# Fused attention and gated MLP on one core: q and k loaded in natural rows, their transposes copied out contiguously, Pool and sync queues in program order

## The chip, the cores and the metric

The kernel runs on one core of a Trainium2 chip. Times are device microseconds of that core, from the first instruction to the last with a little around them; the span in a profile is the stretch between the first and the last recorded instruction. TensorE (PE) multiplies, ScalarE (ACT) and VectorE (DVE) read the results out of PSUM, GpSimd (POOL) works in SBUF only, and SyncE (SP) issues transfers.

## The reference, cut to what matters

There are 8 batches, 8 heads, 512 local and 32 global positions, and a head width of 64. Local queries see the 32 global keys and the local keys at a distance of at most 32; global queries see all keys. The output of the attention, 4352 rows of 512, goes through an MLP of width 2048.

```python
s_ll = scale * np.matmul(q_l, k_l.transpose(0, 1, 3, 2))
mask = np.abs(pos[:, None] - pos[None, :]) <= window        # window = 32
s_ll = np.where(mask, s_ll, -1000000000.0)
s_lg = scale * np.matmul(q_l, k_g.transpose(0, 1, 3, 2))
a_l = sm(np.concatenate([s_lg, s_ll], axis=-1))
out_l = np.matmul(a_l, np.concatenate([v_g, v_l], axis=2))
out_g = np.matmul(sm(scale * np.matmul(q_g, k_all.transpose(0, 1, 3, 2))), v_all)
...
h = x @ w_in
g = h * np.clip(h + 3.0, 0.0, 6.0) / 6.0
out = g @ w_out
```

## The kernel before, in words

**The work is cut into 32 pairs.** A pair `p` is two heads of a batch: batch `b = p // 4`, pair `m = p % 4` of the batch. Heads of a pair share the 128 partitions, 64 each.

- `load_rows` (L93) brings q and k from HBM as fp32. Partition `p` of `kf` and `qf` holds, for each head, the four rows `4p` to `4p + 3`, which lie side by side in HBM: one contiguous run of 1024 bytes for each partition and head. One transfer brings 8 heads of one tensor, 1 MB. The tiles have two buffers.
- `cast_rows` (L121) turns the two heads of a pair into fp16, as `kr` and `qr`, with the fourth `j` of each partition's rows as the outer dimension.
- `emit_T` (L197) transposes `kr` and `qr` on PE in eight 128x128 pieces into one PSUM bank `psT`. Piece `j` holds rows `j, 4 + j, 8 + j, ...`, so that the copies out of PSUM, three on DVE for `kT` (L212) and one on ACT for `qT` (L215), read runs and write every fourth fp16 element.
- `emit_QK` (L220) makes the scores: five small products with the global queries (`psG`, L229) and two PSUM tiles for each head (`psS`, L239), in five chunks of keys. ACT takes the exponential (L242, L244), DVE multiplies with the mask (L245, L247).
- `emit_AV` (L253) multiplies with v, whose tile `vn` has 64 columns of ones beside each head, so that the sums of the softmax arise in the same product (`pav`, L272; `pg` for the global queries, L274). ACT takes the logarithm of the sums (L276) and the exponential of its negative (L279), DVE multiplies (L282). After the last pair of a batch eight DVE multiplications write the global rows `xg` (L292).
- `emit_globals` (L182) transposes the global q and k of a batch (L187) and copies them out on DVE (L190) and ACT (L193).

**The MLP of a batch runs one batch later, in units between the parts of the attention.** `moe_units` (L296) makes 16 units `u1` (four matmuls of 512 columns, L302; a ReLU on ACT, L306; one DVE operation into `gt`, L308) and 16 units `u2` (four matmuls, L317; after every fourth unit a DVE copy `ot`, L321, and a store, L323). `M(n)` issues the next n units. In a pair stand 8 units, in the last of a batch 6 and the rest, so that pairs 0 and 1 of a batch hold the `u1` of the batch before, pairs 2 and 3 its `u2`. After batch 7 its units and those of the 256 global rows run alone.

**What sets the order.** The loop at L368 writes for each pair: loads of the next batch, `emit_T(p + 2)`, the casts of the next batch's pair `m`, `emit_globals(b + 1)` at `m == 1`, one unit, `emit_QK(p + 1)`, four units, `emit_AV(p)` with one unit inside, two units. A scheduler then orders every engine's instructions by its own estimate. It may hoist a transfer on the POOL or SP queue ahead of work written earlier. Weights (`load_w_in` L335, `load_w_out` L340), v (`load_v` L128) and the global q and k (`load_g` L115) come through POOL's queue, which casts fp32 to fp16 on the way; q, k, the v of batch 0 (`load_v0` L135, cast by `cast_v0` L139) and all stores go through SP's. PSUM has 7 general banks (`psp`) and one for `pg`.

Of the kernel before, what the change touches and what calls it, by code (L numbers as in the profile page):

```python
# [14 lines left out]
def kernel(  # L15
# [12 lines left out]
    nc = tc.nc  # L28
    P = 128
# [7 lines left out]
    J = 4  # L37
# [55 lines left out]
    def load_rows(eng, t, src, h0, nh):  # L93
        eng.dma_start(out=t[:, h0:h0 + nh].rearrange("p h j d -> p h (j d)"),  # L94
                      in_=src[h0:h0 + nh].rearrange("h (p j) d -> p h (j d)", j=J))

# [8 lines left out]
    def new_nat(b):  # L105
        f = [natp.tile([P, H, J, D], FP32, tag=t, name=t) for t in ("kf", "qf")]
        nat[b] = (f, {})

    def load_qk(b):
        new_nat(b)  # L110
        for i, src in enumerate((k_l, q_l)):
            load_rows(nc.sync, nat[b][0][i], src[b], 0, H)
# [8 lines left out]
    def cast_rows(b, m, copies):  # L121
        f, r = nat[b]
        r[m] = [natp.tile([P, J, 2, D], FP16, tag=f"{t}{m}", name=f"{t}{m}") for t in ("kr", "qr")]
        for i in range(2):
            copies[i](out=r[m][i],
                      in_=f[i][:, 2 * m:2 * m + 2].rearrange("p h j d -> p j h d"))
# [25 lines left out]
    for i, src in enumerate((k_l, q_l)):  # L152
        load_rows(nc.sync, nat[0][0][i], src[0], 4, 4)
# [43 lines left out]
    def emit_T(p):  # L197
        b, m = divmod(p, NM)
        psT = ps_tile("psT", FP16)
        for w, t in enumerate(nat[b][1][m]):  # L200
            for j in range(J):
# [8 lines left out]
        kv = psT[:, 0:Sl].rearrange("d (j p) -> d j p", j=J)  # L210
        for k0, k1, c0 in SEG:
            nc.vector.tensor_copy(  # L212
                out=kT[:, c0:c0 + k1 - k0].rearrange("d (p j) -> d j p", j=J),
                in_=kv[:, :, k0 // J:k1 // J])
        nc.scalar.copy(  # L215
            out=qT.rearrange("d (p j) -> d j p", j=J),
            in_=psT[:, Sl:2 * Sl].rearrange("d (j p) -> d j p", j=J))
# [32 lines left out]
    xg = [const(f"xg{m}", [P, B, Sg]) for m in range(NM)]  # L250
    pgs = {}

    def emit_AV(p, mid):  # L253
# [29 lines left out]
        if m == NM - 1:  # L283
# [5 lines left out]
            for mm in range(NM):  # L289
                for e in range(2):  # L290
                    r = slice(e * D, (e + 1) * D)
                    nc.vector.tensor_tensor(out=xg[mm][r, b], in0=Rg[r, mm], in1=pg[0:D, mm, e],  # L292
# [134 lines left out]
```

## Time and profile before

| what | value |
|---|---|
| median of 3 runs | 392.61 us (391.6 to 395.03) |
| the profiled execution | 392.18 us, its span 390.5 us |
| span up to the first scores of batch 2 (pair 8) | 98.1 us |
| batches 2 to 6 | 41.5 us each |
| batch 7 | 39.3 us |
| the MLP alone at the end | 45.6 us |
| PE, DVE, ACT, POOL busy | 337.8, 273.8, 270.4, 86.4 us |
| mean granted TensorE clock | 0.989 |

The stages begin where PE issues `psG` of a batch's first pair. A busy PE is not a PE at its peak, since matmuls overlap; where PE waits, the rows of the timeline say for whom, in square brackets. Transfers are split into packets; the view of the transfers counts the packets of each queue in a stretch of time, q0 being POOL's queue and q1 being SP's.

### The profile page before, as it was taken

How to read it: one execution, taken by the hardware profiler on the slowest of the kernel's cores; microseconds unless marked ns; L12 is line 12 of the kernel's file. 1: busy time of each engine (PE TensorE's matmuls, PEld its weight loads, DVE VectorE, ACT ScalarE, POOL GpSimd, SP SyncE). 2: the span in 40 equal slices, each digit the busy share in tenths (PEclk: the TensorE clock that was granted, in tenths of full speed). 3: DMA queues.
4: the chain of work that ended last, by engine and by line, in shares of the span. 5: the costliest groups of instructions: out<-in, count | busy, mean ns of one | idle time of the engine just before them, and what ended most of it. 6: DMA issues, size and time to landing. Idle time of an engine off the chain costs nothing.

```text
span 390.5 us, 6834 instructions
## 1 busy us (share of the span) xinstructions
PE 337.8 (87%) x2560; PEld 186.0 (48%) x2560; DVE 273.8 (70%) x628; ACT 270.4 (69%) x479; POOL 86.4 (22%) x134
## 2 busy tenths in 40 slices
PE   0346686899998999899989999899989998999994
PEld 0224454455454545455545555454545454544472
DVE  4648787966886588857876587668865887276271
ACT  1259896966897589856994799668975897275070
POOL 4057424913321162116211520022000000000000
PEclk9999979999999999999999999999999999999998
DMA  8999999982970195219201660029001100200202
GB/s 168 208 225 274 274 247 179 238 249 62 90 222 10 60 108 164 60 55 98 31 1 43 76 62 2 27 62 87 3 8 60 44 0 2 81 29 0 81 29 54
DMA packets 72274, 36.82 MB, mean 94 GB/s; under 512 B 47408, under 2 KB 67888, under 8 KB 72240
## 3 DMA queue, kind: packets, MB, share of 16 engines
q0 software_dynamic: 44656, 9.25, 26.8%
q1 hardware_dynamic: 27584, 27.14, 22.7%
q8 instruction: 20, 0.33, 0.3%
q14 instruction: 14, 0.11, 0.1%
HBM read 36.70 MB, written 8.91 MB: 117 GB/s over the span
## 4 chain that ended last, share of the span: by engine, by line
PE 41%; ACT 20%; DVE 17%; DMA 11%; issue 5%; SPq 5%; POOL 0%; ACTq 0%
PE po L317 28%; DMA gz_79<-in_k_g_dram 6%; PE psH L302 6%; DVE kT L212 4%; ACT qT L215 4%; ACT Ln L276 4%; SPq L137 4%; PE pav L272 3%; DVE gt L308 3%; DMA qf<-in_q_l_dram 3%; ACT Rc L279 2%; DMA vf<-in_v_l_dram 2%; ACT E L244 1%; SPq L94 1%; PE psT L202 1%
## 5 line engine op out<-in xcount | busy, mean ns | idle before, releaser
L317 PEld LDWEIGHTS <-gt 128*128 128x128 f16 x544 | 49.4, 97 | 54.1 <-issue 2.5
L245 DVE TENSOR_TENSOR E<-E,mask 128x480 f16<-128x480 f16 x128 | 53.6, 439 | 17.9 <-ACT E L244 16.8
L276 ACT ACTIVATE Ln<-pav 64x512 f32<-64x512 f32 x64 | 38.0, 593 | 30.4 <-PE pav L272 23.9
L215 ACT COPY qT<-psT 128x512 f16<-128x512 f16 x32 | 41.8, 1305 | 13.2 <-DVE kT L212 12.5
L212 DVE COPY kT<-psT 128x128 f16<-128x128 f16 (+2 forms) x96 | 41.4, 562 | 5.2 <-PE psT L202 5.2
L321 DVE COPY ot<-po 128x512 f32<-128x512 f32 x34 | 23.4, 689 | 19.0 <-PE po L317 18.6
L317 PE MATMUL po<-wout_91,gt 128*128 128x512 f16 x136 | 35.0, 379 | 0.0
L317 PE MATMUL po<-wout_90,gt 128*128 128x512 f16 x136 | 34.9, 379 | 0.0
L317 PE MATMUL po<-wout_93,gt 128*128 128x512 f16 x136 | 34.9, 379 | 0.0
L317 PE MATMUL po<-wout_92,gt 128*128 128x512 f16 x136 | 34.9, 378 | 0.0
L239 PEld LDWEIGHTS <-kT 64*128 64x128 f16 x320 | 14.7, 98 | 24.8 <-issue 15.8
L242 ACT ACTIVATE Eg<-psG 128x320 f16<-128x320 f32 x32 | 14.1, 439 | 12.5 <-PE psG L229 12.4
L272 PE MATMUL pav<-E,vn_84 128*128 128x160 f16 (+3 forms) x160 | 22.1, 274 | 0.0
L279 ACT ACTIVATE Rc<-Ln 128x512 f32<-128x512 f32 x32 | 20.1, 630 | 0.7
L272 PE MATMUL pav<-E,vn_85 128*128 128x160 f16 (+3 forms) x160 | 20.3, 244 | 0.0
L302 PEld LDWEIGHTS <-win_89 128*128 128x128 f16 x144 | 13.6, 98 | 13.6 <-issue 1.6
L272 PEld LDWEIGHTS <-vn_84 128*128 128x128 f16 x160 | 15.9, 108 | 7.9 <-issue 1.1
L302 PEld LDWEIGHTS <-win_86 128*128 128x128 f16 x144 | 13.5, 98 | 12.9 <-issue 0.9
L302 PEld LDWEIGHTS <-win_87 128*128 128x128 f16 x144 | 13.6, 98 | 12.0
L302 PEld LDWEIGHTS <-win_88 128*128 128x128 f16 x144 | 13.1, 97 | 12.2 <-issue 0.2
L274 PE MATMUL pg<-Eg,vn_84 128*128 128x32 f16 x160 | 13.3, 181 | 6.3 <-DVE vn_84 L140 4.3
L272 PEld LDWEIGHTS <-vn_85 128*128 128x128 f16 x160 | 14.7, 97 | 6.9
(976 smaller groups left out, 831.7 us busy)
## 6 DMA issues: line engine op xcount, KB each, us to landing
out_dram<-ot SPq DMA_DIRECT2D x32, 256.0 KB, 2.0
kf<-in_k_l_dram SPq DMA_DIRECT2D x7, 1024.0 KB, 6.1
qf<-in_q_l_dram SPq DMA_DIRECT2D x7, 1024.0 KB, 9.0
vn_85<-in_v_l_dram POOLq DMA_DIRECT2D x12, 128.0 KB, 4.4
vn_84<-in_v_l_dram POOLq DMA_DIRECT2D x9, 128.0 KB, 3.8
vf<-in_v_l_dram SPq DMA_DIRECT2D x6, 128.0 KB, 6.7
vn_85<-in_v_l_dram POOLq DMA_DIRECT2D x8, 96.0 KB, 4.1
vn_84<-in_v_l_dram POOLq DMA_DIRECT2D x6, 96.0 KB, 4.2
```

The costliest lines, as they stand in the source:

```text
L137: nc.sync.dma_start(out=vf[r0:r1, c, 4 * i:4 * i + 4], in_=src)
L212: nc.vector.tensor_copy(out=kT[:, c0:c0 + k1 - k0].rearrange("d (p j) -> d j p", j=J), in_=kv[:, :, k0 // J:k1 // J])
L215: nc.scalar.copy(out=qT.rearrange("d (p j) -> d j p", j=J), in_=psT[:, Sl:2 * Sl].rearrange("d (j p) -> d j p", j=J))
L239: nc.tensor.matmul(out=pss[e][:, c0:c0 + nq], lhsT=kT[r, KC[c]:KC[c] + P], rhs=qT[r, q0:q0 + nq])
L242: nc.scalar.activation(out=Eg, in_=psG[:, 0:NCH * 2 * Sg], func=EXP, scale=qk_scale)
L245: nc.vector.tensor_tensor(out=E[:, e, t], in0=E[:, e, t], in1=mask[:, t], op=mult)
L272: nc.tensor.matmul(out=pav[:, q0:q0 + nq], lhsT=lhs, rhs=E[:, e, t, c0:c0 + nq], start=(i == 0), stop=(i == NCH - 1), skip_group_check=True)
L276: nc.scalar.activation(out=Ln[e * D:(e + 1) * D], in_=pav[D:P, 0:Sl], func=LN)
L279: nc.scalar.activation(out=Rc, in_=Ln, func=EXP, scale=-1.0)
L302: nc.tensor.matmul(out=ps[:, 0:n], lhsT=w_in_t[c // 4][:, m, (c % 4) * P:(c % 4 + 1) * P], rhs=rhs(m), start=(m == 0), stop=(m == NM - 1))
L317: nc.tensor.matmul(out=po[t][:, 0:dm], lhsT=gts[c][:, t * P:(t + 1) * P], rhs=w_out_t[c // 4][:, c % 4], start=(c == 0), stop=(c == NC - 1))
L321: nc.vector.tensor_copy(out=ot, in_=po[t][:, 0:dm])
```

## The change

- **q and k.** For batches 1 to 7 a tile is loaded in four transfers of 128 rows each. Partition `p` of piece `kb` holds row `128 kb + p` of all heads; the contiguous run in HBM is one row of one head, 256 bytes. `emit_T` then finds the keys in order, and the copies of `kT` and `qT` read and write contiguous runs. Batch 0 keeps the old form. `kf` and `qf` have one buffer in place of two.
- **Queues.** `manual_schedule` for POOL and SP: these two keep the order in which the program is written. The loads of `w_in` stand behind the casts of the v of batch 0, and those of `w_out` behind the v of batch 1. The first v of batch 0 is cast on POOL (DVE before) and loaded ahead of the heads 2 and 3 of q and k. All casts of batch 1 stand on POOL, ahead of the loop (the first two pairs on DVE and ACT before). `load_qk(b + 2)` is written in the last pair of batch `b`, behind the casts of batch `b + 1`.
- **Units and transposes.** `emit_T(4)`, `emit_T(5)` and `emit_QK(4)` move from the last pairs of batch 0 to the start of batch 1, between five units of batch 0's MLP. `emit_globals(b + 1)` stands at `m == 2` of a batch in place of `m == 1`.
- **xg.** One tile in place of four; two DVE multiplications of 64x128 in place of eight of 64x32.

```diff
+    ctx.enter_context(tc.manual_schedule(engines={mybir.EngineType.Pool, mybir.EngineType.SP}))
...
+    def load_rows(b, i, h0, nh):
+        src = (k_l, q_l)[i][b, h0:h0 + nh]
+        t = nat[b][0][i]
+        if b == 0:
+            nc.sync.dma_start(out=f_runs(t)[:, h0:h0 + nh].rearrange("p h j d -> p h (j d)"),
+                              in_=src.rearrange("h (p j) d -> p h (j d)", j=NT))
+        else:
+            for kb in range(NT):
+                nc.sync.dma_start(out=f_rows(t)[:, kb, h0:h0 + nh],
+                                  in_=src[:, kb * P:(kb + 1) * P, :].rearrange("h s d -> s h d"))
...
-        f = [natp.tile([P, H, J, D], FP32, tag=t, name=t) for t in ("kf", "qf")]
+        f = [natp.tile([P, NT * H * D], FP32, tag=t, name=t, bufs=1) for t in ("kf", "qf")]
...
-    for m in range(2):
-        for i, src in enumerate((k_l, q_l)):
-            load_rows(nc.sync, nat[0][0][i], src[0], 2 * m, 2)
-        if m == 0:
-            load_g(0, gf0)
+    for i in range(2):
+        load_rows(0, i, 0, 2)
+    load_g(0, gf0)
     load_v0(0)
-    for i, src in enumerate((k_l, q_l)):
-        load_rows(nc.sync, nat[0][0][i], src[0], 4, 4)
+    for i in range(2):
+        load_rows(0, i, 2, 2)
+    for i in range(2):
+        load_rows(0, i, 4, 4)
     load_v0(1)
...
+        else:
+            for k0, k1, c0 in SEG:
+                nc.vector.tensor_copy(out=kT[:, c0:c0 + k1 - k0], in_=psT[:, k0:k1])
+            nc.scalar.copy(out=qT, in_=psT[:, Sl:2 * Sl])
...
-            for mm in range(NM):
-                for e in range(2):
-                    r = slice(e * D, (e + 1) * D)
-                    nc.vector.tensor_tensor(out=xg[mm][r, b], in0=Rg[r, mm], in1=pg[0:D, mm, e],
-                                            op=mult)
+            for e in range(2):
+                r = slice(e * D, (e + 1) * D)
+                nc.vector.tensor_tensor(out=xg[r, :, b], in0=Rg[r], in1=pg[0:D, :, e], op=mult)
...
     load_qk(1)
-    cast_v0(nc.vector, 0)
+    cast_v0(nc.gpsimd, 0)
+    load_w_in(0)
+    load_w_in(1)
     cast_v0(nc.gpsimd, 1)
-    for i in range(4):
-        load_w_in(i)
+    load_w_in(2)
+    load_w_in(3)
     cast_rows(0, 2, first)
     cast_rows(0, 3, first)
+    load_g(1)
     cast_v0(nc.gpsimd, 2)
     cast_v0(nc.gpsimd, 3)
     nc.vector.memset(vn[1][:, :, :, D:P], 1.0)
-    load_g(1)
     load_v(1)
     for i in range(NC // 4):
         load_w_out(i)
+    for m in range(NM):
+        cast_rows(1, m, pool)
...
-        if b >= 1 and b + 1 < B and m == 0:
-            load_qk(b + 1)
+        if m == 0 and b >= 1 and b + 1 < B:
             load_g(b + 1)
             load_v(b + 1)
-        if p + 2 < NPAIR:
+        if p == NM:
+            M(2)
+            emit_globals(1)
+            emit_T(p)
+            M(1)
+            emit_T(p + 1)
+            M(1)
+            emit_QK(p)
+            M(1)
+            load_qk(2)
+        if m == 2 and 1 <= b < B - 1:
+            emit_globals(b + 1)
+        if p + 2 < NPAIR and p not in (NM - 2, NM - 1):
             emit_T(p + 2)
-        if b + 1 < B:
-            cast_rows(b + 1, m, first if b == 0 and m < 2 else pool)
-        if m == 1 and b + 1 < B:
-            emit_globals(b + 1)
+        if 1 <= b < B - 1:
+            cast_rows(b + 1, m, pool)
+            if m == NM - 1 and b + 2 < B:
+                load_qk(b + 2)
         M(1)
-        if p + 1 < NPAIR:
+        if p + 1 < NPAIR and p != NM - 1:
             emit_QK(p + 1)
```

**How the order moves, in three places.** On POOL at the start of the program, before the change, with `win` the tiles of `w_in`, `vf` the fp32 v of batch 0 and `vn` its fp16 tile:

```order
masks.py:197 MEMSET ident 128x128
L336 DMA win_86<-in_moe_w_in_dram 128x4x512
masks.py:199 ISA
masks.py:199 AFFINE_SELECT ident<-ident 128x128
L159 AFFINE_SELECT mbase<-mbase 128x352
L336 DMA win_87<-in_moe_w_in_dram 128x4x512
L161 AFFINE_SELECT mbase<-mbase 128x352
L336 DMA win_88<-in_moe_w_in_dram 128x4x512
L336 DMA win_89<-in_moe_w_in_dram 128x4x512
L140 CAST vn_84<-vf 128x5x2x64
```

The same place in the changed kernel:

```order
L174 AFFINE_SELECT mbase<-mbase 128x352
L176 AFFINE_SELECT mbase<-mbase 128x352
L155 CAST vn_86<-vf 128x5x2x64
L353 DMA win_88<-in_moe_w_in_dram 128x4x512
L353 DMA win_89<-in_moe_w_in_dram 128x4x512
L155 CAST vn_86<-vf 128x5x2x64
L353 DMA win_90<-in_moe_w_in_dram 128x4x512
L353 DMA win_91<-in_moe_w_in_dram 128x4x512
L131 DMA gz_82<-in_k_g_dram 32x8x64
L131 DMA gz_82<-in_q_g_dram 32x8x64
L155 CAST vn_86<-vf 128x5x2x64 x2
```

All four weight loads stood ahead of the first cast; now the first two stand behind it, and the cast waits for the first half of v.

On SP behind the last part of the v of batch 0, before the change (`ot` is an output tile):

```order
L137 DMA vf<-in_v_l_dram 128x4x64
L94 DMA kf<-in_k_l_dram 128x8x256
L94 DMA qf<-in_q_l_dram 128x8x256
L94 DMA kf<-in_k_l_dram 128x8x256
L94 DMA qf<-in_q_l_dram 128x8x256
L94 DMA kf<-in_k_l_dram 128x8x256
L94 DMA qf<-in_q_l_dram 128x8x256
L94 DMA kf<-in_k_l_dram 128x8x256
L94 DMA qf<-in_q_l_dram 128x8x256
L94 DMA kf<-in_k_l_dram 128x8x256
L94 DMA qf<-in_q_l_dram 128x8x256
L323 DMA out_dram<-ot 128x512 x4
```

The same place in the changed kernel:

```order
L152 DMA vf<-in_v_l_dram 128x4x64
L108 DMA kf<-in_k_l_dram 128x8x64 x4
L108 DMA qf<-in_q_l_dram 128x8x64 x4
L108 DMA kf<-in_k_l_dram 128x8x64 x4
L108 DMA qf<-in_q_l_dram 128x8x64 x4
L340 DMA out_dram<-ot 128x512 x3
L108 DMA kf<-in_k_l_dram 128x8x64 x4
L108 DMA qf<-in_q_l_dram 128x8x64 x4
L340 DMA out_dram<-ot 128x512 x3
```

Five batches of q and k stood ahead of the first store; now two stand there, and from then on each batch's q and k stand behind three stores, with a transfer in four pieces.

On ACT around the copies of the global queries (`qgz`) that batch 3 uses, before the change. The row with `t_1462` is a ReLU of a `u1` unit:

```order
L244 ACTIVATE E<-psS_1433 128x480
L215 COPY qT<-psT 128x4x128
L193 CAST qgz_78<-psGT 64x4x32 x2
L244 ACTIVATE E<-psS_1446 128x480
L244 ACTIVATE E<-psS_1447 128x480
L306 ACTIVATE t_1462<-psH,half_col 128x512
```

The corresponding copies in the changed kernel:

```order
L261 ACTIVATE Eg<-psG 128x320
L263 ACTIVATE E<-psS_1586 128x480
L208 CAST qgz_80<-psGT 64x4x32 x2
L263 ACTIVATE E<-psS_1587 128x480
L236 COPY qT<-psT 128x512
L263 ACTIVATE E<-psS_1600 128x480
L263 ACTIVATE E<-psS_1601 128x480
L295 ACTIVATE Ln<-pav 64x512 x2
```

They leave a pair with ReLUs (pair 1 of the batch before) for one without (its pair 2), and the copy of `qT` has become a contiguous one.

More of the change, by code (lines that the diff above doesn't have):

```diff
@@ L145 @@
     new_nat(0)
[L146 to L150 removed]
+    for i in range(2):
+        load_rows(0, i, 0, 2)
+    load_g(0, gf0)
     load_v0(0)
[L152 to L153 removed]
+    for i in range(2):
+        load_rows(0, i, 2, 2)
+    for i in range(2):
+        load_rows(0, i, 4, 4)
     load_v0(1)
@@ L200, in emit_T @@
         for w, t in enumerate(nat[b][1][m]):
-            for j in range(J):
+            for j in range(NT):
                 nc.tensor.matmul(out=psT[:, w * Sl + j * P:w * Sl + (j + 1) * P],
@@ L249 @@
     xts = {}
-    xg = [const(f"xg{m}", [P, B, Sg]) for m in range(NM)]
+    xg = const("xg", [P, NM, B, Sg])
     pgs = {}
@@ L346 @@
     nc.vector.tensor_copy(out=gz[0][0:Sg], in_=gf0)
-    cast_rows(0, 1, first)
     emit_globals(0)
@@ L350 @@
     emit_masks()
+    cast_rows(0, 1, first)
     emit_T(1)
```

33 lines of the change are left out of this document (17 added, 16 removed).

## The prediction

> **What bounds the kernel now.** I read the page's totals first, then busy time by stages.
>
> ```profile
> span 390.5 us, 6834 instructions
> PE 337.8 (87%) x2560; PEld 186.0 (48%) x2560; DVE 273.8 (70%) x628; ACT 270.4 (69%) x479; POOL 86.4 (22%) x134
> ```
>
> The shares of the whole span name PE, and say nothing of where it waits. So next the stages, cut where PE issues `psG` of a pair; the columns are length, busy time of PE, weight load, DVE, ACT and POOL, granted clock, share of the transfer engines and GB/s.
>
> ```profile
> 0.00:46.70 46.70, 19.93 (x199) 14.26 (x200) 30.08 (x78) 25.56 (x45) 21.64 (x36) 1.00 1.16 228
> 46.70:98.10 51.40, 44.24 (x341) 24.62 (x341) 39.07 (x83) 38.37 (x70) 21.69 (x34) 0.93 1.00 198
> 98.10:108.70 10.60, 9.97 (x85) 5.57 (x84) 9.49 (x24) 10.06 (x17) 4.21 (x7) 1.00 0.85 76
> 108.70:119.30 10.60, 10.09 (x77) 5.46 (x76) 8.47 (x22) 9.79 (x19) 2.08 (x5) 1.00 0.72 204
> 119.30:130.00 10.70, 9.63 (x75) 5.15 (x74) 7.28 (x17) 6.42 (x11) 1.16 (x3) 1.00 0.07 27
> 130.00:139.60 9.60, 9.52 (x77) 5.15 (x76) 5.73 (x14) 6.08 (x12) 3.67 (x6) 1.00 0.40 71
> 139.60:181.10 41.50, 39.21 (x310) 21.31 (x309) 30.98 (x74) 32.34 (x57) 11.12 (x18) 1.00 0.51 94
> 305.60:344.90 39.30, 37.07 (x263) 19.26 (x262) 26.25 (x56) 26.90 (x48) 0.00 (x0) 1.00 0.07 28
> 344.90:390.50 45.60, 40.60 (x219) 21.31 (x218) 23.52 (x47) 17.92 (x32) 0.00 (x0) 0.98 0.12 41
> ```
>
> Three kinds of stage show. A start that fills the transfer engines (share 1.16 and 1.00), with a lowered clock at its end. Batches of 41.5 us, of which the fourth pair takes 9.6 us and the first three 10.6 to 10.7; in the first two ACT is busy 10.06 and 9.79 of 10.6 us. And a tail of MLP alone. What a pair costs PE alone is read from its timeline, in an undisturbed stretch and in a disturbed one:
>
> ```profile
> 128.70 0.39 PE L202 MATMUL psT<-ident,kr_1399 128*128 128x128 f16 x4
> 129.14 1.03 PE L317 MATMUL po<-wout_90,gt 128*128 128x512 f16 x4
> 130.01 0.31 PE L229 MATMUL psG<-qgz_78,kT 128*128 128x64 f16 x5
> 130.90 0.39 PE L317 MATMUL po<-wout_91,gt 128*128 128x512 f16 x1
> 134.36 0.25 PE L272 MATMUL pav<-E,vn_84 128*128 128x192 f16 x1
> 134.90 1.02 PE L317 MATMUL po<-wout_91,gt 128*128 128x512 f16 x4
> 135.76 0.25 PE L272 MATMUL pav<-E,vn_84 128*128 128x192 f16 x1
> ...
> 108.70 0.31 PE L229 MATMUL psG<-qgz_77,kT 128*128 128x64 f16 x5
> 109.64 0.23 PE L239 MATMUL psS_1433<-qT,kT 64*128 64x160 f16 x1 [0.45 <-DVE gt L308]
> ```
>
> From start to start: transposes 0.44 us, a unit 0.865 (0.87 and 0.86), the scores 0.89, one head of AV 0.54. A pair with its eight units costs 8 x 0.865 + 0.44 + 0.89 + 2 x 0.54 = 9.33 us, a batch four times that and 0.2 for the globals, 37.5 us. So 4.0 us of each 41.5 are lost, nearly all where the scores of pairs 0 to 2 wait for a PSUM bank: the last row waits for DVE's `gt`, and DVE's `gt` waits for its turn behind an ACT that is busy for 95% of the pair. In these stages ACT sets the pace, with PE 12% behind.
>
> **The evacuations.** The groups by form, in batch 2:
>
> ```profile
> L215 ACT COPY qT<-psT 128x512 f16<-128x512 f16 x4 | 5.2, 1306 | 1.8 <-DVE kT L212 1.8
> L276 ACT ACTIVATE Ln<-pav 64x512 f32<-64x512 f32 x8 | 4.7, 593 | 3.4 <-PE pav L272 2.5 <-PE pg L274 0.8
> L212 DVE COPY kT<-psT 128x224 f16<-128x224 f16 x4 | 2.8, 697 | 0.0
> L321 DVE COPY ot<-po 128x512 f32<-128x512 f32 x4 | 2.8, 688 | 0.1
> L212 DVE COPY kT<-psT 128x160 f16<-128x160 f16 x4 | 2.2, 555 | 0.0
> L212 DVE COPY kT<-psT 128x128 f16<-128x128 f16 x4 | 1.7, 436 | 0.0
> L193 ACT CAST qgz_78<-psGT 64x128 f16<-64x128 f32 x2 | 0.6, 308 | 0.0
> L292 DVE TENSOR_TENSOR xg_140<-Rg,pg 64x32 f16<-64x32 f32 x2 | 0.4, 182 | 0.0
> L190 DVE CAST kgT_76<-psGT 128x128 f16<-128x128 f32 x1 | 0.3, 314 | 0.0
> ```
>
> ACT reads 512 elements out of PSUM in 593 ns when it writes a run, and needs 1306 for `qT`, which writes every fourth element. No row shows a contiguous fp16 copy out of PSUM. Bounds: 0 us saved (the cost is not in the stride) to 0.71 (it becomes a `Ln`); I take 0.65, since every other ACT row of this width lies near 0.6. On DVE the contiguous rows give (688 - 314) / 384 = 0.97 ns per element and 0.19 us fixed; three contiguous copies are then 3 x 0.19 + 512 x 0.00097 = 1.07 us against 0.697 + 0.555 + 0.436 = 1.69. Bounds 0 to 1.1 saved (only the fixed part stays); I take 0.62. The `qT` copy also waits 0.45 us for `kT` (1.8 over 4), which shrinks with it.
>
> Moving `emit_globals` takes two `qgz` of 0.31 us from ACT in pair 1 to pair 2, where ACT is busy 6.42 of 10.7 us. `xg` goes from 8 x 0.18 = 1.46 us to 2 x 0.31 = 0.63 at the seam of two batches.
>
> ACT in pair 0: 10.06 - 0.65 = 9.4 us; in pair 1: 9.79 - 0.65 - 0.62 = 8.5. PE needs 9.33 and so takes over. I put pair 0 at 9.9 (the two engines are level, so some waiting stays), pair 1 at 9.5, pair 2 at 9.7 (its loss is DVE's backlog from pair 1, plus the globals), pair 3 at 9.6 as now: **38.7 us a batch, 2.8 less**. Bounds: 1.0 less (only the globals and `xg`) to 4.0 less (PE's 37.5). Batch 7, whose last pairs prepare nothing, goes from 39.3 to 37.2. The tail has none of the edited work: 45.6 stays.
>
> **The start.** Here transfers decide, and what a packet costs. Three stretches of the transfer view: fp32 rows of 256 bytes nearly alone on SP's queue (19 to 20 us), the same against weights (15 to 18), and 1024-byte q and k against v (36 to 46):
>
> ```profile
> q1 hardware_dynamic: 767, 0.19, 88.2%
> ...
> q0 software_dynamic: 479, 0.47, 92.9%
> q1 hardware_dynamic: 478, 0.12, 30.1%
> ...
> q1 hardware_dynamic: 2427, 2.44, 88.1%
> q0 software_dynamic: 2424, 0.30, 46.3%
> ```
>
> The counts are equal wherever both queues have work: they take turns packet by packet, 159 pairs per us against weights, 243 for v with 1024-byte rows. Alone, 256-byte packets run at 767 per us. A batch of q and k becomes 2 x 4 x 128 x 8 = 8192 packets instead of 2048, so alone 10.7 us; against v I take 380 pairs per us (half of 767; not below 243).
>
> Now the batch 0 chain. Today the first v lands late and the first weight-fed unit starts at 51.2 us, and globals of batch 2 are late too:
>
> ```profile
> 23.68 0.99 POOL L140 CAST vn_84<-vf 128x640 f16<-128x640 f32 x1 [17.96 <-DMA vf<-in_v_l_dram]
> 51.23 0.63 PE L302 MATMUL psH<-xt_319,win_86 128*128 128x512 f16 x1
> 65.75 0.42 PE L187 MATMUL psGT<-ident,gz_79 128*128 128x32 f16 x7 [2.88 <-DMA gz_79<-in_k_g_dram]
> ```
>
> With the weights behind it, the first half of v (2560 packets behind 512 large and 512 small ones) lands near 8.5 us, and weights start near 11.5. They, 2048 packets, then alternate with the second half of v, 2560 packets: 28 us. Batch 0 on ACT alone (four pairs of about 5 us from 14) ends near 37 instead of 50. But q and k of batch 1 start only behind that v: 3 us alone, then 5120 pairs with v of batch 1 at 380, 13.5 us, and the rest against `w_out`: q complete at 47, cast and transposed at 48. PE has two units to do meanwhile and sits idle from about 39. So the wait for the first v becomes a wait for q of batch 1. From 48 the batch still owes two units and transposes (2.3 us), 28 units and four pairs (28 x 0.865 + 4 x 2.41 = 33.9), 1.5 of waiting, and a cold start: the clock row 0.93 of 51.4 us is 3.6 us lost after today's thin stretch; I take 2.6. Then q of batch 2: issued at 50 behind POOL's casts, it shares with the rest of `w_out` and with v of batch 2 and lands near 74, where PE asks at 71: 3 us. Sum 48 + 2.3 + 33.9 + 1.5 + 2.6 + 3 = 91, less about 1 because the reordered units fill part of that: **90 us for what now takes 98.1**. Bounds: 82 (q of batch 1 at 42, nothing late after) and 98 (at 52, batch 2 late by 6).
>
> [...]
>
> **Costed at nothing.** The first casts of batch 1 on POOL instead of DVE and ACT: POOL is busy 21.6 of the first 46.7 us. One buffer and program order on SP: `load_qk(b + 2)` stands behind stores of pair 2 and waits for casts that POOL made at the start of the batch; behind it stand the stores of pairs 3 and 0, for which only `ot` copies wait, four buffers deep. It is issued three pairs, 29 us, before its transposes and needs about 11 to 14 plus 1 for cast. If that cover goes, each microsecond late costs one per batch.
>
> **Sum.** 90 + 5 x 38.7 + 37.2 + 45.6 = 366.3 us of span, against 390.5. The profiled execution took 392.18, 1.7 more than its span and 0.4 less than the median: **368 us**.
>
> **Rivals.**
> - *The evacuations stay as slow.* Then a batch gains 1.0 us, 6 in all: 392.2 - 8 - 6 = 378. For it: no contiguous fp16 row exists. Against: 593 and 688 beside 1306 and 1688. Chance 0.08. [...]
> - *The start gives nothing.* q of batches 1 and 2 come so late that 98 stays: 392.2 - 5 x 2.8 - 2.1 = 376. For it: the start is full of transfers, and PE's transposes stand in order ahead of units that could run. Against: today's start has its own idle stretches. Chance 0.13.
> - *Packets cost by number, not size: slower.* At the 58 ns of a 1024-byte packet (0.881 x 16 x 10 us / 2427) a batch of q and k takes 8192 x 58 / 16 = 29.7 us, over the 29 it has; with landing and cast the transposes are 4.5 late, a batch takes 43.2, 10 us more in all, and the start loses 12 against today: 414. It decides from about 45 ns. Against: 0.882 x 16 us / 767 = 18 ns. Chance 0.08.
>
> **Numbers.** The forecast has 0.71. Its own span is 355 (82 at the start, 37.5 a batch: 354) to 376; with the first two rivals the range is 355 to 381. Faster by over 1%, about the least that a measurement of this kernel can tell from no change: 0.90; within it 0.02; slower 0.08.
>
> **What would show it.** `qT` near 0.65 us and the `kT` copies near 1.07 together; ACT busy about 30 us in a batch of 38.7; the scores of pairs 0 and 1 without long waits. First v cast near 9 us, an idle PE between 39 and 48 that waits for `qr` of batch 1, scores of pair 8 at 90. The forecast is wrong if `qT` stays over 1 us, if PE waits for `qr` after batch 2, or if pair 8 starts after 98.

## The result, and the profile after

The changed kernel takes 377.27 us (median of 4 runs, 373.02 to 379.06) against 393.46 (391.6 to 395.03): a ratio of 0.952, 95% interval 0.942 to 0.962. The ratio counts only the changed kernel's two fast runs, 375.87 and 373.02 us, and not the slow ones of 378.68 and 379.06. Its profiled execution took 375.87 us with a span of 374.2, 16.3 less than before. The forecast was 368 with a range of 355 to 381: the side and the range held. Where 24 us less were forecast, the medians and the profiled executions give about 16, the ratio gives 19.

One name has to be mended first. The mark that the table and the prediction call the first scores of batch 2, pair 8, is the tenth `psG` group, so the scores of pair 9, which the loop issues in its turn for pair 8. The stages are cut at the same group in both kernels, so their lengths stand; a "pair" of a stage below is a turn of the loop.

The page's totals and the stages of the changed kernel (length, busy time of PE, weight load, DVE, ACT and POOL, granted clock, share of the transfer engines, GB/s):

```profile
span 374.2 us, 6794 instructions
PE 331.2 (89%) x2560; PEld 182.8 (49%) x2560; DVE 247.2 (66%) x577; ACT 249.6 (67%) x477; POOL 88.2 (24%) x139
```

```profile
0.00:53.40 53.40, 25.09 (x220) 17.24 (x221) 30.67 (x83) 28.35 (x52) 22.01 (x38) 0.81 1.17 195
53.40:91.50 38.10, 36.95 (x319) 20.96 (x318) 26.90 (x71) 28.91 (x57) 12.07 (x20) 1.00 0.82 128
132.30:142.10 9.80, 9.44 (x76) 5.08 (x75) 8.43 (x19) 9.43 (x17) 7.54 (x14) 1.00 1.45 172
142.10:152.50 10.40, 9.90 (x86) 5.46 (x85) 8.78 (x20) 9.54 (x17) 0.52 (x1) 1.00 0.11 8
152.50:162.40 9.90, 9.54 (x76) 5.14 (x75) 5.91 (x19) 5.21 (x11) 0.00 (x0) 1.00 0.07 26
162.40:172.00 9.60, 9.52 (x77) 5.13 (x76) 5.18 (x13) 5.34 (x12) 2.48 (x4) 1.00 0.78 178
132.30:172.00 39.70, 38.40 (x310) 20.82 (x309) 28.30 (x68) 29.52 (x57) 10.54 (x18) 1.00 0.59 94
```

Against the sum of the prediction:

| stage | before | forecast | measured |
|---|---|---|---|
| to the scores of pair 9 | 98.1 | 90 | 91.5 |
| batches 2 to 6 | 5 x 41.5 | 5 x 38.7 = 193.5 | 40.7 + 4 x 39.74 = 199.7 |
| batch 7 and the MLP at the end | 84.9 | 82.8 | 83.0 |

So 6.2 of the 7.9 us that the span is longer than forecast (374.2 against 366.3) lie in the batches, and there mostly in the second pair: 10.4 us where 9.5 were forecast.

The groups by form, in the batch from 132.3 us:

```profile
L236 ACT COPY qT<-psT 128x512 f16<-128x512 f16 x4 | 2.4, 588 | 0.2 <-DVE kT L235 0.2
L235 DVE COPY kT<-psT 128x224 f16<-128x224 f16 x4 | 1.1, 265 | 0.0
L235 DVE COPY kT<-psT 128x160 f16<-128x160 f16 x4 | 0.9, 232 | 0.0
L235 DVE COPY kT<-psT 128x128 f16<-128x128 f16 x4 | 0.9, 216 | 0.0
```

The copies became cheaper than forecast: `qT` 0.59 us (forecast 0.65), the three `kT` together 0.71 (forecast 1.07). The gain is smaller all the same.

The waits of PE up to 92 us, summed by line and releaser, and POOL's casts in that stretch:

```profile
PE psT L217 <- POOL qr_273 L139: 7.8, 1, 7.8
...
PE psT L217 <- POOL kr_272 L139: 2.4, 1, 2.4
```

```profile
8.80 0.72 POOL L155 CAST vn_86<-vf 128x640 f16<-128x640 f32 x1 [6.40 <-DMA vf<-in_v_l_dram]
...
49.16 0.62 POOL L139 CAST qr_273<-qf 128x512 f16<-128x512 f32 x1 [7.79 <-DMA qf<-in_q_l_dram]
```

As forecast, the first v is cast at 8.8 us instead of 23.7, and the long wait of the start is now one for q of batch 1.

### The profile page after: what moved, and what is told of

Read it like the earlier page. It is cut to its first block, busy times and chain, and to the rows that moved or that the text cites. A ratio compares the mean times of both kernels' runs of the same rounds, so it can differ in the third digit from the quotient of the medians.

```text
span 374.2 us, 6794 instructions
## 1 busy us (share of the span) xinstructions
PE 331.2 (89%) x2560; PEld 182.8 (49%) x2560; DVE 247.2 (66%) x577; ACT 249.6 (67%) x477; POOL 88.2 (24%) x139
## 3 DMA queue, kind: packets, MB, share of 16 engines
q0 software_dynamic: 44656, 9.25, 27.9%
## 4 chain that ended last, share of the span: by engine, by line
PE 45%; ACT 29%; DVE 15%; issue 5%; DMA 4%; SPq 1%; POOL 0%; ACTq 0%; DVEq 0%; POOLq 0%
PE po L334 28%; PE psH L319 7%; ACT E L263 6%; ACT Ln L295 6%; PE pav L291 4%; DVE gt L325 4%; DMA qf<-in_q_l_dram 4%; ACT Rc L298 3%; ACT qT L236 2%; PE psT L217 2%; DVE kT L229 1%; DVE kT L235 1%; ACT Eg L261 1%; SPq L108 1%; PE pg L293 1%
## 5 line engine op out<-in xcount | busy, mean ns | idle before, releaser
L264 DVE TENSOR_TENSOR E<-E,mask 128x480 f16<-128x480 f16 x128 | 51.4, 413 | 10.9 <-ACT E L263 7.7
L145 POOL DMA_DIRECT2D vn_87<-in_v_l_dram x20 | 17.0, 861 | 69.7 <-PE pg L293 54.6
L145 POOL DMA_DIRECT2D vn_86<-in_v_l_dram x15 | 12.8, 861 | 51.2 <-PE pg L293 50.1
L291 PE MATMUL pav<-E,vn_86 128*128 128x160 f16 (+3 forms) x160 | 23.6, 273 | 0.2 <-ACT Eg L261 0.2
L258 PEld LDWEIGHTS <-kT 64*128 64x128 f16 x320 | 13.6, 96 | 20.6 <-issue 18.0
L235 DVE COPY kT<-psT 128x128 f16<-128x128 f16 (+2 forms) x84 | 16.1, 238 | 11.3 <-PE psT L217 11.2
L291 PE MATMUL pav<-E,vn_87 128*128 128x160 f16 (+3 forms) x160 | 21.3, 244 | 0.0
L319 PEld LDWEIGHTS <-win_88 128*128 128x128 f16 x144 | 13.7, 100 | 15.1 <-issue 4.0
L298 ACT ACTIVATE Rc<-Ln 128x512 f32<-128x512 f32 x32 | 20.1, 628 | 0.7
L319 PEld LDWEIGHTS <-win_90 128*128 128x128 f16 x144 | 13.3, 98 | 13.1 <-issue 1.2
L319 PEld LDWEIGHTS <-win_89 128*128 128x128 f16 x144 | 13.0, 97 | 12.8 <-issue 1.0
L319 PEld LDWEIGHTS <-win_91 128*128 128x128 f16 x144 | 13.0, 97 | 12.2 <-issue 0.2
L291 PEld LDWEIGHTS <-vn_86 128*128 128x128 f16 x160 | 16.2, 107 | 5.6 <-issue 0.8
L293 PE MATMUL pg<-Eg,vn_87 128*128 128x32 f16 x160 | 18.6, 178 | 0.0
```

What stands on the lines that cost most here:

```text
L145: nc.gpsimd.dma_start(out=vn[b % NV][r0:r1, c, :, 0:D], in_=src)
L235: nc.vector.tensor_copy(out=kT[:, c0:c0 + k1 - k0], in_=psT[:, k0:k1])
L264: nc.vector.tensor_tensor(out=E[:, e, t], in0=E[:, e, t], in1=mask[:, t], op=mult)
L291: nc.tensor.matmul(out=pav[:, q0:q0 + nq], lhsT=lhs, rhs=E[:, e, t, c0:c0 + nq], start=(i == 0), stop=(i == NCH - 1), skip_group_check=True)
L293: nc.tensor.matmul(out=pg[:, m, e], lhsT=lhs, rhs=Eg[:, c, e * Sg:(e + 1) * Sg], start=(i == 0), stop=(i == NCH - 1), skip_group_check=True)
L298: nc.scalar.activation(out=Rc, in_=Ln, func=EXP, scale=-1.0)
```

## The experiments

Each stands against the changed kernel. "Pair 9" is the start of its scores, "batch" the mean length of batches 3 to 6, all from profiled executions; ratios are to the kernel before, with 95% intervals.

| kernel | span | pair 9 | batch | ratio |
|---|---|---|---|---|
| before | 390.5 | 98.1 | 41.5 | 1 |
| changed | 374.2 | 91.5 | 39.7 | 0.952 (0.942 to 0.962) |
| strided copies | 394.5 | 98.7 | 41.6 | 0.997 (0.992 to 1.001) |
| long runs | 370.9 | 83.2 | 40.4 | 0.954 (0.950 to 0.957) |
| globals early | 373.6 | 91.2 | 39.7 | 0.957 (0.953 to 0.960) |
| qT on DVE | 373.1 | 90.9 | 39.7 | 0.957 (0.954 to 0.960) |
| spread units | 371.2 | 86.0 | 39.2 | 0.960 (0.954 to 0.967) |
| batch 1 in long runs | 368.8 | 86.3 | 39.7 | 0.945 (0.940 to 0.950) |
| weights first | 371.3 | 88.7 | 39.7 | 0.953 (0.950 to 0.956) |
| transposes behind the scores | 373.2 | 90.8 | 39.7 | 0.956 (0.954 to 0.958) |
| seam undone | 381.5 | 100.0 | 39.7 | 0.983 (0.976 to 0.990) |
| mixed units | 376.0 | 79.9 | 39.5 | 0.965 (0.962 to 0.968) |
| mixed, batch 1 in long runs | 375.0 | 79.0 | 39.5 | 0.957 (0.953 to 0.962) |
| spread, batch 1 in long runs | 368.0 | 84.3 | 39.2 | 0.940 (0.938 to 0.942) |

The whole time differs by some us from run to run of one kernel. The batches 3 to 6 agree within 0.1 us among the changed kernel and the kernels whose edit lies only in the start (weights first, seam undone, batch 1 in long runs), so the batch questions are read from batch lengths. The start has one profiled execution of each kernel, and its landing of q differs from execution to execution (see the last point on the prediction). In the spread and the mixed kernels units move from batch 1 to the MLP at the end, so an early pair 9 is in part only work put off: with spread units the end behind batch 6 takes 85.5 us, in the changed kernel 83.0.

### What a batch gains

**Strided copies.**

```diff
-        if b == 0:
+        if True:
             kv, qv = ...
```

> The changed kernel with the copies of kT and qT of all batches writing every fourth fp16 element again, as in batch 0; loads, queues and units stay. The loaded rows lie in another order than these copies assume, so keys and queries come out permuted; the work is the same. Theory A (ACT's own work in the pairs with u1 units sets a batch): qT goes from 0.59 back to 1.31 us and kT from 0.71 to 1.69, ACT gets 0.72 us in each of the two u1 pairs, and a batch goes from 39.7 to 41.0 to 41.2, 8 us in all. Rival B (the stride costs nothing, the copies became faster through the way the rows are loaded): qT stays at 0.59 and the batch at 39.7. Rival C (PE is the bound in these pairs): a batch moves by less than 0.5.

The batch came to 41.6 us, the length of before. Its groups by form:

```profile
L232 ACT COPY qT<-psT 128x512 f16<-128x512 f16 x4 | 5.2, 1304 | 1.6 <-DVE kT L229 1.6
L229 DVE COPY kT<-psT 128x224 f16<-128x224 f16 x4 | 2.8, 697 | 0.0
```

With the new loads in place the old durations return, so the stride alone made the difference in the copies, and without their gain nothing of a batch's gain is left: 1.9 us (41.6 - 39.7). `emit_globals` and `xg` do not show in the length. They did move time, though: PE's wait of 0.6 us for `xg` in the first pair is gone, and with strided copies this pair takes 9.9 us against 10.6 before the change, but the second takes 11.4 against 10.6. What `xg` is worth with contiguous copies was not run. PE's row before the change:

```profile
99.55 0.45 PE L274 MATMUL pg<-Eg,vn_84 128*128 128x32 f16 x8 [0.63 <-DVE xg_140 L292]
```

The lost time stands in the second and third pair (11.4 and 10.7 against 10.4 and 9.9), not in the first (9.9 against 9.8). B and C fall. The strides cost more than A's 1.3 to 1.5, so A's own sum was not right either. (This execution, 396.16 us, is the longest of the kernel's seven, of which the shortest took 389.24, and q of batch 1 was cast late, at 52.8 us; so its span and its start are not compared. The granted clock of the batches read here is 1.00.)

**Globals early.**

```diff
-        if m == 2 and 1 <= b < B - 1:
-            emit_globals(b + 1)
 ...
+        if m == 1 and 1 <= b < B - 1:
+            emit_globals(b + 1)
         M(1)
```

> The changed kernel with emit_globals(b + 1) at m == 1 again. Theory A (ACT is full in both u1 pairs, 9.54 us of 10.4 in the second): two qgz copies, 0.52 us, come into the full pair, and a batch goes from 39.7 to about 40.1; pair 1 gets longer by 0.4 to 0.6 and pair 2 shorter by 0.1 to 0.2. Rival (the prediction's picture, by which ACT has a us to spare in pair 1): 39.7 stays within 0.1.

39.7: theory A fails. Its pairs, from the stages:

```profile
131.90:141.90 10.00, 9.64 (x84) 5.29 (x83) 8.59 (x19) 9.43 (x17) 7.88 (x14) 1.00 1.43 169
141.90:152.30 10.40, 10.04 (x78) 5.38 (x77) 8.71 (x22) 10.02 (x19) 0.17 (x1) 1.00 0.11 8
152.30:162.00 9.70, 9.36 (x76) 5.12 (x75) 5.83 (x16) 4.75 (x10) 0.00 (x0) 1.00 0.07 27
```

ACT is now busy 10.02 of 10.4 us in the second pair and the pair is no longer than with 9.54. Only PE's 0.2 us of transposes changed its pair. The result agrees with the rival's number but not with its reason, since ACT had no microsecond to spare here.

**qT on DVE.**

```diff
-            nc.scalar.copy(out=qT, in_=psT[:, Sl:2 * Sl])
+            (nc.vector.tensor_copy if m >= 2 else nc.scalar.copy)(
+                out=qT, in_=psT[:, Sl:2 * Sl])
```

> The changed kernel with the qT copy of the two transposes that fall into the u1 pairs (those of pairs 2 and 3 of a batch) on DVE in place of ACT. ACT loses 0.59 us in each u1 pair, DVE gains about 0.6 to 0.69. Theory A (ACT's work sets the u1 pairs): a batch goes from 39.7 to 38.8 to 39.2. Rival B (DVE's order, which frees the PSUM banks for the scores, sets them): a batch gets longer, 40.2 to 40.8. Neither (PE or PSUM banks alone): within 0.2 of 39.7.

39.7 again, with 9.25 us of ACT in the second pair instead of 9.54. More work on ACT (globals early) does not move the batch, so ACT's load over a pair is not what sets it. Less work on ACT together with more on DVE doesn't either, though here the two could have cancelled.

So I looked at what the scores wait for. PE in the second pair, then DVE in the same stretch:

```profile
142.93 0.29 PE L258 MATMUL psS_2030<-qT,kT 64*128 64x320 f16 x1 [0.19 <-DVE gt L325]
143.52 0.29 PE L258 MATMUL psS_2031<-qT,kT 64*128 64x320 f16 x1 [0.30 <-DVE gt L325]
```

```profile
140.76 1.40 DVE L301 TENSOR_TENSOR xt_1918<-Rc,pav 64x512 f16<-64x512 f32 x2 [0.59 <-ACT Rc L298]
142.18 0.69 DVE L325 SCALAR_TENSOR_TENSOR gt<-t_1967,psH 128x512 f16<-128x512 f32 x1
142.79 0.68 DVE L325 SCALAR_TENSOR_TENSOR gt<-t_1976,psH 128x512 f16<-128x512 f32 x1
143.39 0.55 DVE L235 COPY kT<-psT 128x128 f16<-128x128 f16 x3
143.85 0.68 DVE L325 SCALAR_TENSOR_TENSOR gt<-t_2005,psH 128x512 f16<-128x512 f32 x1
```

The scores need five PSUM banks at once (one for `psG`, four for `psS`). The units just ahead of them hold theirs until DVE's `gt`, and DVE does these in its order, behind the two `xt`, which wait for ACT's `Rc` of the last product with v; `kT` and the third `gt` queue behind. As I read the rows, this is a chain from one matmul to the next, and not an engine that is full over the pair: DVE is busy 8.78 of 10.40 us, though without a gap from 140.76 past 145, and ACT without one from 136.80 to 142.0. The third pair waits the same way. The first waits for `ot`, which stands on DVE behind `xt` and `xg`:

```profile
133.38 0.29 PE L258 MATMUL psS_1873<-qT,kT 64*128 64x320 f16 x1 [0.36 <-DVE ot L338]
```

In the four pairs of this batch the scores take 1.41, 1.71, 1.52 and 0.89 us from their first matmul to the next unit; the fourth has only `u2` units ahead. With 0.25 us at the seam the excess over 0.89 is 2.2 us, all that a batch of 39.7 loses against PE's 37.5.

**Transposes behind the scores.**

```diff
-        if p + 2 < NPAIR and p not in (NM - 2, NM - 1):
+        if p + 2 < NPAIR and p < NM - 2:
             emit_T(p + 2)
 ...
             emit_QK(p + 1)
+        if p + 2 < NPAIR and p >= NM:
+            emit_T(p + 2)
```

> The changed kernel with emit_T(p + 2) written behind emit_QK(p + 1) from pair 4 on, in place of ahead of it; all work stays. Theory D (seven PSUM banks: the scores ask for five while psT, two pav and the last psH hold the others): psT no longer stands ahead of the scores, so their stretches of 1.41, 1.71 and 1.52 us shrink to at most 1.2 each, and a batch goes from 39.7 to 38.4 to 39.1. Rival (DVE's and ACT's order alone, whichever bank is asked for): the stretches stay within 0.2 us, and the batch at 39.4 to 39.9.

39.7: the rival's number. Taking `psT` from ahead of the scores brings nothing, so it is not psT's bank that the scores miss.

**Spread units.** The last four `u2` units of a batch are held back:

```diff
+    HOLD = 4
-    def M(n):
+    def M(n, hold=HOLD):
         for _ in range(n):
-            if units:
+            if len(units) > hold:
 ...
-            M(len(units))
-            units += moe_units(...)
+            M(len(units) - HOLD)
+            new = moe_units(...)
+            units[:] = new[:6] + units + new[6:]
```

> The changed kernel with the last four u2 units of each batch held back and put behind the first six u1 units of the next, so that the four pairs of a batch hold 6, 6, 4 and 0 u1 units in place of 8, 8, 0 and 0. PE's work stays the same. Theory D (what is left of the loss, 2.2 us of a batch of 39.7, is the scores' wait for the PSUM banks that u1 units hold until ACT and DVE, each in its order, have read them): fewer units queue ahead of the scores, their stretches of 1.41, 1.71 and 1.52 us shrink toward 0.89, and a batch goes to 38.2 to 38.9; 5 to 9 us in all. Rival (each pair with u1 units pays its 0.5 to 0.8 us whatever their number): three pairs now hold some, and the batch stays at 39.7 or gets up to 0.4 longer.

39.2: between the two; the ratio, 0.960, is no better than the changed kernel's 0.952. Its pairs:

```profile
128.80:138.70 9.90, 9.54 (x78) 5.16 (x76) 8.52 (x19) 8.16 (x15) 8.09 (x14) 1.00 1.43 172
138.70:148.10 9.40, 9.40 (x85) 5.29 (x84) 6.83 (x17) 8.28 (x15) 0.02 (x1) 1.00 0.19 37
148.10:158.50 10.40, 10.02 (x79) 5.37 (x78) 7.93 (x22) 7.53 (x15) 0.00 (x0) 1.00 0.00 0
158.50:168.00 9.50, 9.42 (x75) 5.06 (x74) 5.09 (x13) 5.34 (x12) 2.44 (x4) 1.00 0.96 192
```

The second pair, whose scores now have `u2` units just ahead, takes 9.4 us, the best of any. The third, with `u1` units just ahead of its scores, takes 10.4, and ACT is busy only 7.53 of it. So it is the place of the `u1` units that counts here, more than their number.

**Mixed units.** Each pair holds four `u1` behind its scores, then four `u2` of the batch before that one (`HOLD = NC + 1`, 34 buffers for `gt`):

```diff
+            old, units[:] = units[1:], units[:1]
+            for i in range(4):
+                units.extend(new[4 * i:4 * i + 4] + old[4 * i:4 * i + 4])
+            units.extend(new[NC:])
```

> The changed kernel with every pair holding four u1 units behind its scores and then four u2 units of the batch before that one, so that only u2 units stand directly ahead of the scores; 34 buffers for gt in place of 24. PE's work stays; batch 1 holds about 15 units less and the tail 16 more. Theory D, mended (what is left of the loss is paid where the three units just ahead of the scores are u1 units, whose banks wait for a ReLU and a gt behind Rc and xt): all four stretches of the scores come to 0.8 to 1.0 us, and batches 3 to 6 go from 39.7 to 37.5 to 38.0. With batch 1 shorter and the tail longer by about the same, 364 to 370 in all. Rival (ACT's and DVE's load as such, or the number of banks): a u1 unit costs the scores something wherever it stands, and a batch stays at 38.6 or more.

38.5 us in every second batch, 40.6 in the others. In the short ones the scores take 0.84, 1.18, 1.31 and 1.13 us, and the wait has changed hands: 0.3 to 0.4 us in three of four pairs for a bank that ACT's `qT` frees. So in the short batches 1.2 of the 2.2 us go with the place of the units, and about 1.0 stays. The theory's 37.5 to 38.0 was not reached, and 38.5 lies just under the rival's 38.6: the theory holds by half. The 2.1 us of the longer batches have another cause. DVE's and POOL's rows there:

```profile
163.04 5.39 DVE L264 TENSOR_TENSOR E<-E,mask 128x480 f16<-128x480 f16 x4 [0.21 <-ACT E L263]
```

```profile
163.84 0.66 POOL L139 CAST kr<-kf 128x512 f16<-128x512 f32 x1
164.39 0.66 POOL L139 CAST qr<-qf 128x512 f16<-128x512 f32 x1
...
168.12 0.78 POOL L139 CAST qr<-qf 128x512 f16<-128x512 f32 x1
```

Four mask products of 0.4 us take 5.39 while POOL casts without a gap, one of them alone about 3 (an estimate: 5.39 less three products at 0.8, the time of one beside a cast at 71.21 us of the kernel before). In the short batch from 122.3 us, with the same eight casts, DVE is busy 2.5 us less (29.73 against 32.25); what decides between the two was not found. The whole kernel is no faster than the changed one (ratio 0.965 against 0.952, median 378.47 against 377.27), the pair from 79.9 us taking 13.3 besides.

### What the start gains

**Weights first.**

```diff
+    for i in range(4):
+        load_w_in(i)
     cast_v0(nc.gpsimd, 0)
-    load_w_in(0)
-    load_w_in(1)
     cast_v0(nc.gpsimd, 1)
-    load_w_in(2)
-    load_w_in(3)
```

> The changed kernel with the four loads of w_in ahead of all casts of v on POOL's queue again, the rest as changed. Theory (the start gains only what the gated weights let v and then q of batch 1 land sooner): the first v cast goes back from about 15 to 20 us or later, the pairs of batch 0 go with it, but q of batch 1 still ends the wait, since bytes and packets ahead of it are the same; scores of pair 4 within 2 us of 53.4. Rival (the gating moves the whole start, as the prediction had it: 8 us): scores of pair 9 at 95 to 99 instead of 91.5.

The first cast of v goes back to 20.1 us, the first scores from 12.9 to 21.5, and yet the scores of pair 4 come at 50.6 (53.4 with gated weights) and those of pair 9 at 88.7. What batch 0 loses, q of batch 1 makes good:

```profile
48.38 0.40 PE L217 MATMUL psT<-ident,qr 128*128 128x128 f16 x4 [0.62 <-POOL qr L139]
```

The long wait for q has shrunk to 0.62 us because PE arrives later. The rival, which is the prediction's picture of the start, falls: gating the weights brings nothing, and the ratios agree (0.953 against 0.952). (Pair 4 moved by 2.8 us, a little over the 2 that I allowed. My expectation also named about 15 us for the first cast of v, which the changed kernel does at 8.8.)

**Seam undone.**

```diff
-        if p == NM:
-            M(2)
-            emit_globals(1)
-            emit_T(p)
 ...
-        if p + 2 < NPAIR and p not in (NM - 2, NM - 1):
+        if p + 2 < NPAIR:
             emit_T(p + 2)
 ...
-        if p + 1 < NPAIR and p != NM - 1:
+        if p + 1 < NPAIR:
             emit_QK(p + 1)
+        if p == NM - 1:
+            load_qk(2)
```

> The changed kernel with the transposes of pairs 4 and 5, the scores of pair 4 and the globals of batch 1 back in the last pairs of batch 0, ahead of the units; loads, copies and queues stay. Theory (the start waits for q of batch 1, and what the moved order gains is that PE does units and the last products of batch 0 while it waits): PE stands at the transposes of pair 4 with work of batch 0 and units behind them; the scores of pair 9 go from 91.5 to 95 to 99, a batch stays at 39.7, 4 to 7 us more in all. Rival (the order at this place is worth nothing, since the wait for q is the same): the scores of pair 9 within 1.5 us of 91.5.

Scores of pair 9 at 100.0, past the expected range, and 7.3 us more span. PE around the wait:

```profile
40.62 0.61 PE L217 MATMUL psT<-ident,kr 128*128 128x128 f16 x4 [9.44 <-POOL kr L139]
48.05 0.61 PE L217 MATMUL psT<-ident,qr 128*128 128x128 f16 x4 [6.82 <-POOL qr L139]
48.45 0.47 PE L248 MATMUL psG<-qgz,kT 128*128 128x64 f16 x5
48.86 0.98 PE L258 MATMUL psS<-qT,kT 64*128 64x160 f16 x10
49.77 1.78 PE L291 MATMUL pav<-E,vn 128*128 128x192 f16 x10
```

PE stands at the transposes of pair 4 with scores and products of batch 0 (the rows from 48.45) behind it. Without the moved transposes the start is 1.9 us worse than before the change (100.0 against 98.1), with them 6.6 better: in these executions 8.5 us are the order on PE.

**Batch 1 in long runs.** `b == 0` becomes `b <= 1` in `load_rows`, `cast_rows` and `emit_T`:

```diff
-        if b == 0:
+        if b <= 1:
             nc.sync.dma_start(out=f_runs(t)[...], ...)
```

> The changed kernel with batch 1 too in the form of batch 0: 1024-byte runs and copies that write every fourth element, its results as the reference's. Theory (the start waits for q of batch 1): the scores of pair 4 go from 53.4 to 43 to 45 as in the run with long runs for all, and the scores of pair 9 from 91.5 to 84 to 87, the copies of batch 1 giving some of it back; batches 3 to 6 stay at 39.7; 4 to 7 us less in all. Rival (POOL's casts then fall in a burst on DVE's mask products in batch 2 or later, as in that run): the scores of pair 9 come sooner, but 2 us or more are lost again behind them.

Pair 4 at 45.1, pair 9 at 86.3, batches as they were. POOL casts k at 39.5 and q right behind, where the changed kernel has 49.2:

```profile
39.49 0.70 POOL L139 CAST kr<-kf 128x512 f16<-128x512 f32 x1
```

Of the 8.3 us at pair 4, 3.1 are given back in batch 1 (45.1 to 86.3 is 41.2, against 38.1). How much of that the old copies cost is not shown: the run with long runs for all, whose copies are contiguous, takes 39.4 us there, with a granted clock of 0.57 from 44 to 48 us. The theory holds: behind pair 9 the kernel takes as long as the changed one (282.5 and 282.7 us), so the rival's burst does not show. By the ratios, 0.945 against 0.952, the intervals overlap.

**Long runs for all.** `b == 0` becomes `True` in `load_rows` and `cast_rows`; `emit_T` stays, so the copies are contiguous:

> The changed kernel with q and k of all batches loaded in runs of 1024 bytes, as in batch 0, and the copies contiguous as changed. Keys and queries come out permuted; the work is the same. Theory (the start waits for q of batch 1, whose 8192 packets of 256 bytes take their turns behind v and beside weights and v of batch 1): 2048 packets of 1024 bytes land 9 to 11 us sooner, the transposes of q of batch 1 go from 49.8 to about 40, and the scores of pair 9 from 91.5 to 82 to 86; batches stay at 39.7; 7 to 9 us less in all. Rival (the start is bound by bytes or by other work): the scores of pair 9 stay within 2 us of 91.5.

Pair 9 at 83.2, as forecast. But 3.3 us of span are won in all, not 7 to 9, and by the ratio (0.954 against 0.952) nothing: batches 2 and 6 take 43.1 and 42.1. DVE in batch 6:

```profile
248.35 3.12 DVE L266 TENSOR_TENSOR Eg<-Eg,maskg 128x128 f16<-128x128 f16 x1
251.38 2.27 DVE L264 TENSOR_TENSOR E<-E,mask 128x480 f16<-128x480 f16 x3
```

A product of 0.22 us takes 3.12, under POOL's casts again. q lands soon enough that all eight casts run without a gap at the moment of the mask products; in the changed kernel the late q puts a gap of 1.4 to 2.9 us behind the first cast. The casts alone do not decide it: the next three products, beside the last of the same casts, take 2.27 together (0.4 each usual), and batches 3 to 5, with as many casts, stay at 39.7 to 39.9.

### Together

> The two edits that brought something by themselves, together: batch 1 in runs of 1024 bytes, and the last four u2 units of a batch held back behind six u1 units of the next. Theory (one gain lies in the start, the other in each batch, and they add up): scores of pair 9 near 86 as with the runs alone, batches 3 to 6 at 39.2 as with the spread units alone, 364 to 368 in all, 4 to 7 below the changed kernel's profiled 375.9. Rival (POOL's casts fall on DVE's mask products at the new places and stretch one of them to 3 us, as in the runs with long runs for all and with mixed units): a pair of 11 us or more in some batch, and 368 or more in all.

The spread units with batch 1 in long runs: ratio 0.940 (0.938 to 0.942), 369.24 us, the lowest of all, though its interval overlaps that of batch 1 in long runs alone (0.940 to 0.950). Batches at 39.2 and pair 9 at 84.3, as expected; the whole, with 368.0 of span and 369.7 in the profiled execution, is above the 364 to 368 that I gave, so the two gains don't add up in full. No pair from batch 3 on is over 10.5 us; the first turn of batch 2 takes 12.0. That is over the rival's 11, but likely not for its reason: PE is idle for 2.35 us between 84 and 88 us, and in the spread kernel, where it waits 2.19 us for `qT` at this place, the mask products keep their time (two in 0.72 to 0.98 us). Mixed units with batch 1 in long runs:

> The mixed units together with batch 1 in runs of 1024 bytes. Theory (the two gains lie in different stages and add up): batches 3 to 6 as in the mixed kernel, 37.5 to 38.0, and q of batch 1 cast at about 39.5 instead of 49; batch 1, with fewer units to fill it, may now wait for q of batch 2. In all 359 to 367. Rival (the start hands its gain back, since q of batch 2 lands no sooner than at about 69 to 72): no more than 2 us less than the mixed kernel alone.

375.0 of span, 1.0 less than mixed units alone (by the medians 3.0 less, 375.43 against 378.47): near the rival's 2, and the expected 359 to 367 missed by far. PE there waits 5.6 us for q of batch 2 at 69.6, since batch 1 no longer has units to fill the time.

## Why the prediction was right, and where it wasn't

- **The evacuations.** Right in kind, and the rival "stay as slow" is dead: 1306 to 588 ns for `qT`, 697 to 265 for the widest `kT`. The strided rerun, where `qT` takes 1304 again, shows that the stride alone does it.
- **The batch, 38.7 forecast, 39.7 measured.** The step that failed is "In these stages ACT sets the pace", and with it "9.79 - 0.65 - 0.62 = 8.5. PE needs 9.33 and so takes over". Two errors are in it. ACT's busy time in a pair was taken for the pair's demand; but ACT lags, and work of the second pair was done in the third pair's stretch. The copies shortened ACT by 0.72 us in each pair, yet its busy time, from the batch before the change to the one after, fell by 0.63, 0.25, 1.21 and 0.74 from pair to pair of the batch, although the 0.6 us of `qgz` also moved from the second to the third. And a busy share of 95% was taken for the limit: 0.5 us more of ACT leaves the batch at 39.7, and so does 0.3 less. In its place the rows show the chain from the last product with v over `Ln`, `Rc` and `xt` to the `gt` that frees a bank for the next scores; by it the second pair took 10.4 us where 9.5 were forecast. The spread and the mixed units show that the place of the `u1` units matters; the chain link by link is read from the rows and was not cut by a run of its own. How much of the copies' 1.9 us comes through DVE and how much through ACT was not separated.
- **`emit_globals` and `xg`.** 0.62 us of ACT and 0.8 at the seam were credited. Without the faster copies the two brought nothing: with strided copies the first pair is 0.8 us shorter than before, the second 0.8 longer, and the batch as long. With the faster copies, moving `emit_globals` back changes nothing; `xg` was not undone there.
- **The start, 90 forecast, 91.5 measured.** Right in what PE waits for (`qr` of batch 1, transposes at 49.8 where 48 was forecast) and when. Single terms were off and cancelled, which is luck: the wait for q of batch 2, put at 3 us, does not exist, and the cold start cost about 1.4 instead of 2.6 (granted clock 0.50 from 49.8 to about 52.7). Against that, the work from there to the mark was put at 2.3 + 33.9 = 36.2 us and comes to about 38.4 by the same prices (an estimate): the mark is pair 9, so five sets of scores lie before it and not four, and some more transposes and most of a unit. The last 1.9 of the 41.7 us lie mainly in scores that took up to 1.97 us instead of 0.89. Wrong in the credit: the gain was put down to v that lands sooner behind gated weights, and the reordered units were given about 1 us. The gated weights bring nothing, and the moved transposes and units are worth 8.5; the faster copies in batch 1 bring some part of the 3.1 us that batch 1 in long runs gives back. Against both stands what the wait for q costs.
- **Batch 7 and the tail.** 82.8 forecast, 83.0 measured.
- **Packets by number.** Behind the start nothing of it: no wait for `kr` or `qr` there, and q of each later batch lands in time. In the start the number did cost: q of batch 1 is cast at 49.2 us in 8192 packets of 256 bytes and at 40.0 in 2048 of 1024 (batch 1 in long runs).
- **The spread of the runs.** Up to its cast, q of batch 1 meets the same code in seven of the profiled kernels (changed, strided, globals early, qT on DVE, spread, transposes behind, mixed); its cast there began between 46.0 and 52.8 us. This is likely why the changed kernel spreads over 6 us, but only one execution of it has a trace.

## What to carry to other kernels

A busy share near 95%, read from a stretch in which the engine lags behind, need not be what the stretch demands, nor show that the engine is the limit: look at what the waiting instruction's bank, buffer or operand is held by, and follow that chain through the order in which each engine did its work. A transfer that is brought forward pays only if the instruction that waits longest depends on it; here the late one was q of the next batch, and the order on PE around that wait was worth more than any order of loads. Bursts of casts on POOL came with DVE products stretched by whole microseconds (0.22 to 3.12 us with long runs for all), so that an earlier landing can cost what it saves.

## What the hardware showed that was not expected

- A DVE product of two SBUF operands took 3.12 us (0.22 usual) with long runs for all, at 248.35 us, and 2.67 us (0.40 usual) in the kernel before, at 68.62 us, while POOL cast; `gt` and `xt`, which read PSUM, kept their 0.69 beside such casts (in the changed kernel from 138 to 141.5 us). Other products of 0.4 us took 0.4 to 0.9 beside casts (0.40 at 134.42 us of the changed kernel, 0.92 at 32.90 and 0.81 at 71.21 us of the kernel before, three in 2.27 from 251.38 us with long runs for all). The product of 3.12 us lasted through five casts.
- A short wait of PE could cost more than itself. With spread units PE waited 2.19 us for `qT`, and the granted clock then fell to a half for 3.4 us (0.50 from 89 to 92 us, 0.82 from 92 to 93), so that the turn took 13.5 us against 10.7 in the changed kernel; a wait of 0.91 at the same place of the changed kernel left the clock at 1.00. The length of the idle time alone does not decide: in the spread kernel with batch 1 in long runs PE was idle for 2.35 us between 84 and 88 us, the clock stayed at 1.00 up to 94 us, and the turn took 12.0. The rows of the spread kernel:

```profile
88.84 0.52 PE L258 MATMUL psS<-qT,kT 64*128 64x320 f16 x4 [2.19 <-ACT qT L236]
```

```profile
89.00:92.00 3.00, 2.98 (x11) 1.04 (x8) 2.17 (x7) 2.40 (x7) 2.19 (x4) 0.50 1.69 186
```
